# Chunk-contiguous spectra in a fused Fourier / mixture-of-experts / feed-forward kernel

## The chip, the cores and the metric

The kernel runs on one core of a Trainium2 chip. The metric is the device time of one launch in microseconds (us), as a median over runs. Of the five engines, PE multiplies matrices, ACT and VectorE (DVE) do elementwise work and move results out of the accumulator memory (PSUM), POOL does elementwise work on SBUF alone, and SP issues most of the DMAs. "PEld" is PE's loading of the stationary operand, which overlaps its matmuls.

## The reference, cut to what matters

```python
X = np.fft.rfft(x, axis=1)                      # x: 8 x 3072 x 256
Yr = Xr @ w_r - Xi @ w_i + b_r
Yi = Xr @ w_i + Xi @ w_r + b_i
Y  = sign(Y) * max(|Y| - 0.01, 0)               # real and imaginary part apart
x  = np.fft.irfft(Y, n=3072, axis=1).reshape(24576, 256)
# soft mixture of experts: logits = x @ phi; softmax over tokens (dispatch) and over slots (combine);
# 8 experts of two matrices each on 32 slots; then
h  = x @ w_in;  out = (h * tanh(softplus(h))) @ w_out      # 256 -> 2048 -> 256
```

The change is in the first part, between the Fourier transform and the complex product with `w_r` and `w_i`.

## The kernel before, in words

**Two stretches.** The first, up to some 720 us of the trace, runs the Fourier transform, the complex product with its shrinkage, the inverse transform and the softmaxes of the mixture for all 8 sequences, and converts `w_in` and `w_out` on the side. The second, to the end, is the feed-forward part (`ffn`, L797).

**The first stretch by groups.** A sequence is transformed in two stages. `stage1` (L182) is a matrix product over 128 points, whose result goes to memory and comes back in another order (`load_b`, L209). `stage2` (L215) finishes the transform for a group `k` of 8 pairs of frequency blocks; there are 4 groups to a sequence, so 32 in all. Then `linear(k, eh, m)` (L238) makes the complex product in three real products (`m` = 0, 1, 2, with the weights `a`, `b`, `c`) for each half `eh` of the output features, and shrinks the result: ACT evicts `k1`, DVE adds (`p`, L264), ACT makes two one-sided parts (`cl`, `p`, L270 and L271), POOL subtracts them (`yt`, L272). `project` and `inv1` make the logits' share of the group, `ytrans` turns it for later, and `inv2`, `smax1` to `smax3`, `csoft1`, `csoft2`, `fwd1`, `fwd2`, `dturn`, `slots` and `ctrans` work on the softmaxes of a whole sequence.

**The tiles that the change touches.** `stage2` runs for each half `h` of the input features in chunks that start at `p0` = 0, 3 and 6 and hold 3, 3 and 2 pairs: six chunks to a group. A chunk is one PSUM tile `s2` of `n` pairs by 3 parts (real, imaginary, their sum) by 48 frequencies. ACT rounds it into the tile `xh` (L232, to float32r, the type in which the products of `linear` run), and DVE subtracts that from the chunk and writes the remainder into `xl` (L233). Both tiles hold, per half, part by part: 384 real values, 384 imaginary, 384 sums, and two more columns, which are copies (L236) that only the first group of a sequence has. The writes of a chunk therefore go to three places, 384 columns apart. `linear` reads one part as one run of 384 columns, in six matmuls per product (weights high times `xh`, high times `xl`, low times `xh`, for both halves).

**What sets the order.** Each step is put into a list with a position (`at`), the list is sorted, and the instructions are issued in that order: each engine takes its own in order. `stage2(k)` stands at `k` - 1.1, its six chunks one behind the other, before `linear(k-1)`. Waits between engines are placed by the framework, from the stretches of the tiles that the instructions read and write. All PSUM tiles of this stretch come from one pool of 8 banks (`psp`, L104), so PE can start a new tile only when ACT or DVE has read the tile that held the bank.

Of the kernel before, what the change touches and what calls it, by code (L numbers as in the profile page):

```python
# [8 lines left out]
F32 = mybir.dt.float32  # L9
F32R = mybir.dt.float32r  # L10
# [11 lines left out]
NC = 384  # L22
# [8 lines left out]
def constants():  # L31

    n1 = np.arange(N1, dtype=np.float64)
    n2 = np.arange(N2, dtype=np.float64)
    f1 = np.zeros((N1, N1))
    t = np.zeros((96, NP, 96))
    w = 2.0 * np.pi / SEQ
    for i in range(64):
        p, par = divmod(i, 2)
        m, r0, c0 = 2 * i, par * 48, par * 24  # L40
        q = {0: 1, 1: 0}.get(i, i)
        if q:
            ang = 2.0 * np.pi * np.mod(n1 * q, N1) / N1
            f1[:, m], f1[:, m + 1] = np.cos(ang), -np.sin(ang)
            for k2 in range(N2):
                a = w * np.mod(n2 * (q + 128 * k2), SEQ)
                sg = 1.0 if k2 < 12 else -1.0
                t[r0:r0 + 24, p, c0 + k2] = np.cos(a)
                t[r0 + 24:r0 + 48, p, c0 + k2] = np.sin(a)
                t[r0:r0 + 24, p, 48 + c0 + k2] = -sg * np.sin(a)  # L50
                t[r0 + 24:r0 + 48, p, 48 + c0 + k2] = sg * np.cos(a)
        else:
            f1[:, m], f1[:, m + 1] = 1.0, np.where(n1 % 2 == 0, 1.0, -1.0)
            for pos in range(23):
                k, r = (128 * (pos + 1), r0) if pos < 11 else (64 + 128 * (pos - 11), r0 + 24)
                a = w * np.mod(n2 * k, SEQ)
                t[r:r + 24, p, c0 + pos] = np.cos(a)
                t[r:r + 24, p, 48 + c0 + pos] = -np.sin(a)
            t[r0:r0 + 24, p, c0 + 23] = 1.0
            t[r0:r0 + 24, p, 48 + c0 + 23] = np.where(n2 % 2 == 0, 1.0, -1.0)  # L60
    sel = np.tile(np.eye(NS), (4, 1))
    m = np.arange(128).reshape(4, 4, 2, 4)
    order = m.transpose(1, 0, 2, 3).reshape(-1)
    big = np.concatenate([f1, f1.T[order], np.eye(128), sel], axis=1)
    tt = t.transpose(2, 1, 0)
    t3 = np.concatenate([t, t[:, :, 0:48] + t[:, :, 48:96]], axis=2)
    both = np.concatenate([t3.reshape(96, -1), tt.reshape(96, -1)], axis=1)
    return np.ascontiguousarray(big.astype(np.float32)), np.ascontiguousarray(both.astype(np.float32))

# [2 lines left out]
def body(ctx, tc, x, w_r, w_i, b_r, b_i, phi, w1, w2, w_in, w_out, cbig, ct, out, dbg=None, stop=False):  # L72
    nc = tc.nc
# [26 lines left out]
    bp = ctx_r.enter_context(tc.tile_pool(name="bp", bufs=2, side="right"))  # L100
# [5 lines left out]
    def psum(shape, name):  # L106
        return psp.tile(shape, F32, tag="p", name=name)

    tall = const.tile([96, NP * 240], F32, name="tall")
    t_m = tall[:, 0:NP * 144].rearrange("p (n f) -> p n f", f=144)  # L110
# [6 lines left out]
    wsp = {n: (wp.tile([128, 2, D], F32R, name=n + "h"), wp.tile([128, 2, D], F32R, name=n + "l")) for n in "abc"}  # L117
# [8 lines left out]
    x_t, b_t, xh_t, xl_t, yt_t, y_t, pt_t, k1_t = {}, {}, {}, {}, {}, {}, {}, {}  # L126
# [88 lines left out]
    def stage2(k, h, p0):  # L215
        b, g = divmod(k, 4)
        n = min(3, 8 - p0)
        if h == 0 and p0 == 0:
            xh_t[k] = bp.tile([128, 2, 3 * NC + 2], F32R, tag="xh", name="xh")
            xl_t[k] = bp.tile([128, 2, 3 * NC + 2], F32R, tag="xl", name="xl")  # L220
        full = psum([128, 3, 3, 48], "s2")
        ps = full[:, 0:n]
        for i in range(n):
            nc.tensor.matmul(ps[:, i], lhsT=b_t[k][:, p0 + i, h * 128:(h + 1) * 128], rhs=t_m[:, 8 * g + p0 + i, :],  # L224
                             start=True, stop=True)

        def part(t):
            v = t[:, h, 0:3 * NC].rearrange("p (r q f) -> p q r f", r=3, f=48)
            return v[:, p0:p0 + n]

        xh = part(xh_t[k])
        nc.scalar.activation(out=xh, in_=ps, func=AF.Copy)  # L232
        nc.vector.tensor_sub(part(xl_t[k]), ps, xh.bitcast(F32))  # L233
        if g == 0 and p0 == 0:
            for t in (xh_t[k], xl_t[k]):
                nc.vector.tensor_copy(t[:, h, 3 * NC:3 * NC + 2], t[:, h, 47:48 + NC:NC].bitcast(F32))  # L236

    def linear(k, eh, m):  # L238
        if eh == 0 and m == 0:
            pool, tag = (bp, "b") if k >= NK - 2 else (yq, "yq") if k >= NK - 4 else (ytp, "yt")  # L240
            yt_t[k] = pool.tile([128, 2, 8, 2, 48], F32, tag=tag, name="yt")
        xh, xl, yt = xh_t[k], xl_t[k], yt_t[k]
        src, (wh, wl) = ((2, wsp["a"]), (1, wsp["b"]), (0, wsp["c"]))[m]
        w = NC + 2 if m == 0 and k % 4 == 0 else NC
        full = psum([128, NC + 2], "l")
        ps = full[:, 0:w]
        cs = slice(src * NC, src * NC + w)
        es = slice(eh * 128, eh * 128 + 128)
        n = 0
        for h in range(2):  # L250
            for ww, xx in ((wh, xh), (wh, xl), (wl, xh)):
                nc.tensor.matmul(ps, lhsT=ww[:, h, es], rhs=xx[:, h, cs], start=n == 0, stop=n == 5)  # L252
                n += 1
        if m == 0:
            k1_t[eh] = lp.tile([128, NC + 2], F32, tag="k1", name="k1")
            nc.scalar.activation(out=k1_t[eh][:, 0:w], in_=ps, func=AF.Copy)
            if w > NC:
                cs_t[eh] = cs = sm.tile([128, 2, 2], F32, tag="cs", name="cs")
                for i, sc in ((0, 0.5), (1, -0.5)):
                    nc.scalar.activation(out=cs[:, i], in_=k1_t[eh][:, NC:w], func=AF.Relu, scale=sc, bias=half[:, i, eh:eh + 1])  # L260
            return
        ri = m - 1
        p = lp.tile([128, 8, 48], F32, tag="p", name="p")
        nc.vector.tensor_add(p.rearrange("p q f -> p (q f)"), ps, k1_t[eh][:, 0:NC])  # L264
        cl = lp.tile([128, 8, 48], F32, tag="cl", bufs=1, name="cl")
        if k == NK - 1:
            nc.vector.tensor_scalar(cl, p, tlo[:, ri, eh:eh + 1], thi[:, ri, eh:eh + 1], op0=ALU.max, op1=ALU.min)
            nc.vector.tensor_sub(yt[:, eh, :, ri, :], p, cl)
        else:
            nc.scalar.activation(out=cl, in_=p, func=AF.Relu, bias=tup[:, ri, eh:eh + 1])  # L270
            nc.scalar.activation(out=p, in_=p, func=AF.Relu, scale=-1.0, bias=tlo[:, ri, eh:eh + 1])  # L271
            nc.gpsimd.tensor_sub(yt[:, eh, :, ri, :], cl, p)  # L272
        if m == 2 and k % 4 == 0:
            cs = cs_t.pop(eh)
            nc.gpsimd.tensor_sub(yt[:, eh, 0, :, 47], cs[:, 0], cs[:, 1])
# [177 lines left out]
    def evict(b, v, out, ps):  # L453
        if v:
            nc.vector.tensor_copy(out, ps)
        else:
            nc.scalar.activation(out=out, in_=ps, func=AF.Copy)

    def fwd2(b, g):
        dd = ch[b, 0]  # L460
        ps = psum([128, 2, 96], "dt")
        for i in range(2):
            for j in range(4):
                q = 8 * g + 2 * j + i
                nc.tensor.matmul(ps[32 * j:32 * j + 32, i], lhsT=dd[q], rhs=t_m[:, q, 0:96],
                                 start=True, stop=True, tile_position=(0, 32 * j))
        dt = cp.tile([128, 2, 96], F32, tag="pt", bufs=4, name="dtt")
        evict(b, g % 2, dt, ps)
        ch[b, 7, g] = dt
# [100 lines left out]
    for k in range(NK):  # L570
        at(-4 + 0.01 * k if k < 2 else 2.45 if k == 4 else k + PA["lb"], load_b, k)
        for i, (h, p0) in enumerate((h, p0) for h in range(2) for p0 in (0, 3, 6)):
            at(k + PA["s2"] + PA["s2d"] * i, stage2, k, h, p0)
        for i in range(6):
            at(k + i / 6, linear, k, i // 3, i % 3)
        at(k + PA["pj"], project, k)
        at(k + PA["pj"] + 0.3, inv1, k)
        for c in range(4):
            at(k + PA["yt"] + PA["ytd"] * c if k < NK - 4 else NK + TAIL["yt"][k - NK][c], ytrans, k, c)
# [41 lines left out]
    with tc.manual_schedule():  # L621
# [11 lines left out]
        ps = psum([128, 2, NS], "sip")  # L633
# [292 lines left out]
```

## Time and profile before

| | |
|---|---|
| runs | 1980.21, 1981.95, 1984.83 us (median 1981.95) |
| the profiled execution | 1981.18 us, of which the span from first to last instruction is 1979.4 us |
| PE busy | 1922.4 us (97%) |
| DVE busy | 1173.4 us (59%) |
| ACT busy | 892.9 us (45%) |
| POOL busy | 196.9 us (10%) |
| mean granted clock of PE | 0.993 |

The busy time of PE is that of matmuls whose ends are modelled, and they overlap. What PE waits for is read from its idle time, and where that idle time lies from the stretches.

### The profile page before, as it was taken

The page shows a single profiled execution, that of the slowest core. Times are in us where ns is not written, and L with a number is a line of the kernel's source. Part 1 is how long each engine was busy: PE and PEld are TensorE (multiplying, and loading weights), DVE is VectorE, ACT ScalarE, POOL GpSimd, SP SyncE. Part 2 cuts the span into 40 slices and gives each one's busy share as a digit, 9 for nine tenths or more (in the row PEclk, how much of TensorE's full clock was granted, in tenths as well). Part 3 has the DMA queues.
Part 4 walks back from the last instruction along what each step waited for, and adds up shares of the span by engine and source line. Part 5 has one row for each costly group of instructions (what it writes and reads, how often), then busy time and mean ns, then how long its engine had stood idle before and what let it go on. Part 6 is the DMA issues. An engine that isn't in the chain of part 4 may idle for free.

```text
span 1979.4 us, 30141 instructions
## 1 busy us (share of the span) xinstructions
PE 1922.4 (97%) x12226; PEld 1604.8 (81%) x12226; DVE 1173.4 (59%) x1805; ACT 892.9 (45%) x1444; POOL 196.9 (10%) x247
## 2 busy tenths in 40 slices
PE   8899999999998899999999999999999999999999
PEld 5687777777877668888888888888888888888887
DVE  3345555555565656666666666666666666666665
ACT  2666666667666433333333333333333333333332
POOL 0332332333323100000000000000000000000000
PEclk9999999999999999999999999999999999999999
DMA  8655565555542670010002002002001002000000
GB/s 250 216 144 155 158 174 159 157 168 153 170 130 74 250 240 22 22 50 26 22 12 54 22 22 54 22 22 54 22 22 43 22 22 54 22 22 22 22 22 22
DMA packets 92202, 164.26 MB, mean 83 GB/s; under 512 B 27280, under 2 KB 58640, under 8 KB 90016
## 3 DMA queue, kind: packets, MB, share of 16 engines
q1 hardware_dynamic: 90128, 157.45, 26.4%
q0 software_dynamic: 1792, 4.76, 0.7%
q8 instruction: 96, 1.57, 0.3%
q14 instruction: 42, 0.34, 0.1%
q10 hardware_dynamic: 144, 0.13, 0.0%
HBM read 98.75 MB, written 63.57 MB: 82 GB/s over the span
## 4 chain that ended last, share of the span: by engine, by line
PE 82%; ACT 6%; DVE 5%; issue 3%; DMA 2%; POOL 1%; ACTq 0%; SPq 0%; DVEq 0%; POOLq 0%
PE o L858 54%; PE h L828 9%; PE l L252 6%; PE s L224 4%; PE s L195 3%; DVE xl L233 2%; ACT xh L232 2%; PE tr L305 2%; ACT cl L270 1%; ACT p L271 1%; POOL yt L272 1%; PE sps L488 1%; ACT y L310 1%; PE pp L283 1%; DVE p L264 1%
## 5 line engine op out<-in xcount | busy, mean ns | idle before, releaser
L858 PE MATMUL o<-whl,gh 128*128 128x512 f32 x3072 | 1082.9, 395 | 0.0
L858 PE MATMUL o<-whl,gl 128*128 128x256 f32 x3072 | 827.8, 280 | 0.0
L834 ACT ACTIVATE g<-h 128x1024 f32<-128x1024 f32 x384 | 394.3, 1027 | 746.3 <-PE h L828 739.3
L858 PEld LDWEIGHTS o<-whl,gh 128*128 128x128 f32 x3072 | 566.5, 188 | 121.5
L858 PEld LDWEIGHTS o<-whl,gl 128*128 128x128 f32 x3072 | 578.5, 188 | 31.5
L843 DVE TENSOR_TENSOR gl<-g,gh 128x1024 fp32r<-128x1024 f32 x384 | 470.2, 1225 | 28.8 <-DVE gh L839 0.9
L839 DVE CAST gh<-g 128x1024 fp32r<-128x1024 f32 x384 | 265.9, 693 | 351.9 <-ACT g L834 351.8
L828 PE MATMUL h<-ctt,mst 128*128 128x512 f32 x768 | 240.8, 395 | 0.0
L233 DVE TENSOR_TENSOR xl<-s,xh 128x432 fp32r<-128x432 f32 (+1 forms) x192 | 106.1, 558 | 169.2 <-ACT xh L232 169.2
L272 POOL TENSOR_TENSOR yt<-cl,p 128x384 f32<-128x384 f32 x124 | 125.4, 1011 | 399.6 <-ACT p L271 314.3
L224 PE MATMUL s<-tall,bt 96*128 96x144 f32 x1024 | 136.5, 293 | 9.9 <-DMA bt<-sdr 5.4
L224 PEld LDWEIGHTS s<-tall,bt 96*128 96x128 f32 x1024 | 134.7, 197 | 13.7 <-issue 12.2
L232 ACT ACTIVATE xh<-s 128x432 fp32r<-128x432 f32 (+1 forms) x192 | 90.8, 490 | 115.0 <-DVE xl L233 75.9
L828 PEld LDWEIGHTS h<-ctt,mst 128*128 128x128 f32 x768 | 121.2, 188 | 17.9 <-DVE mst L815 0.5
L866 DVE TENSOR_TENSOR os<-o,os 128x256 f32<-128x256 f32 x192 | 76.7, 420 | 77.0 <-ACT os L865 77.0
L270 ACT ACTIVATE cl<-p,tup 128x384 f32<-128x384 f32 x124 | 76.3, 616 | 97.2 <-DVE p L264 69.3
L195 PE MATMUL s<-xc,cb 128*128 128x512 f32 x192 | 104.0, 633 | 8.2 <-DMA xc<-in_x_dram 7.6
L264 DVE TENSOR_TENSOR p<-l,k 128x384 f32<-128x384 f32 x128 | 70.5, 553 | 61.4 <-PE l L252 37.4
L865 ACT ACTIVATE os<-o 128x256 f32<-128x256 f32 x192 | 73.7, 384 | 41.6 <-PE o L858 37.7
L271 ACT ACTIVATE p<-p,tlo 128x384 f32<-128x384 f32 x124 | 76.3, 616 | 4.0
L305 PE MATMUL tr<-cb,yt 128*96 128x128 f32 x512 | 66.6, 276 | 2.9 <-DVE xl L233 1.6
L305 PEld LDWEIGHTS tr<-cb,yt 128*96 128x96 f32 x512 | 53.8, 126 | 18.8 <-DVE xl L233 7.1
(185 smaller groups left out, 1495.8 us busy)
## 6 DMA issues: line engine op xcount, KB each, us to landing
bt<-sdr SPq DMA_DIRECT2D x32, 768.0 KB, 8.0
out_dram<-os SPq DMA_DIRECT2D x47, 512.0 KB, 2.6
xc<-in_x_dram SPq DMA_DIRECT2D x42, 512.0 KB, 5.3
sdr<-a SPq DMA_DIRECT2D x42, 512.0 KB, 3.2
ctt<-c_d SPq DMA_DIRECT2D x28, 384.0 KB, 7.2
c_d<-chl SPq DMA_DIRECT2D x16, 384.0 KB, 3.1
w1t<-in_moe_w_dram SPq DMA_DIRECT2D x6, 1024.0 KB, 6.8
w2t<-in_moe_w_dram SPq DMA_DIRECT2D x5, 1024.0 KB, 10.8
```

The source lines that it names most:

```text
L195: nc.tensor.matmul(ps, lhsT=f1, rhs=xs, start=True, stop=True)
L224: nc.tensor.matmul(ps[:, i], lhsT=b_t[k][:, p0 + i, h * 128:(h + 1) * 128], rhs=t_m[:, 8 * g + p0 + i, :], start=True, stop=True)
L232: nc.scalar.activation(out=xh, in_=ps, func=AF.Copy)
L233: nc.vector.tensor_sub(part(xl_t[k]), ps, xh.bitcast(F32))
L252: nc.tensor.matmul(ps, lhsT=ww[:, h, es], rhs=xx[:, h, cs], start=n == 0, stop=n == 5)
L272: nc.gpsimd.tensor_sub(yt[:, eh, :, ri, :], cl, p)
L305: nc.tensor.transpose(ps[:, i, eh], yt[:, eh, 2 * c + i].rearrange("p r f -> p (r f)"), ident)
L828: nc.tensor.matmul(ps[:, i], lhsT=mst[:, f * 128:f * 128 + 128], rhs=ct_t[b][:, 4 * m:4 * m + 4].rearrange("p n t -> p (n t)"), start=True ...
L834: nc.scalar.activation(out=g, in_=h_t.pop(p), func=AF.Mish)
L839: nc.vector.tensor_copy(gh, g)
L843: nc.vector.tensor_sub(gl, g, gh.bitcast(F32))
L858: nc.tensor.matmul(o, lhsT=a[:, i, ts], rhs=w, start=f == 0 and n == 0, stop=f == 15 and n == 1)
```

## The change

The spectra `xh` and `xl` are laid out with the pair outermost, then the part, then the frequency, where before the part was outermost. A chunk of `stage2` now writes one run of 432 (or 288) columns. The parts stand in the order sum, real, imaginary, for which the constants are put in that order too (`t3`), and `fwd2` reads its two parts from column 48 on. `linear` reads a part as 8 runs of 48 columns, 144 apart, through an access pattern written by hand. The two extra columns become a ninth run of 48, filled with 24 copies of the two values, so the product with `a` in the first group of a sequence has 432 columns where it had 386. The scratch space for POOL's DMAs is halved, as the tiles grow by 46 columns in each half.

```diff
-    t3 = np.concatenate([t, t[:, :, 0:48] + t[:, :, 48:96]], axis=2)
+    t3 = np.concatenate([t[:, :, 0:48] + t[:, :, 48:96], t], axis=2)
...
-            xh_t[k] = bp.tile([128, 2, 3 * NC + 2], F32R, tag="xh", name="xh")
-            xl_t[k] = bp.tile([128, 2, 3 * NC + 2], F32R, tag="xl", name="xl")
+            xh_t[k] = bp.tile([128, 2, 3 * NC + 48], F32R, tag="xh", name="xh")
+            xl_t[k] = bp.tile([128, 2, 3 * NC + 48], F32R, tag="xl", name="xl")
...
         def part(t):
-            v = t[:, h, 0:3 * NC].rearrange("p (r q f) -> p q r f", r=3, f=48)
-            return v[:, p0:p0 + n]
+            return t[:, h, 144 * p0:144 * (p0 + n)].rearrange("p (q r f) -> p q r f", r=3, f=48)
...
-                nc.vector.tensor_copy(t[:, h, 3 * NC:3 * NC + 2], t[:, h, 47:48 + NC:NC].bitcast(F32))
+                nc.vector.tensor_copy(t[:, h, 3 * NC:3 * NC + 48].rearrange("p (a r) -> p a r", r=2),
+                                      t[:, h, 95:144:48][:, None, :].to_broadcast([128, 24, 2]).bitcast(F32))
...
-        src, (wh, wl) = ((2, wsp["a"]), (1, wsp["b"]), (0, wsp["c"]))[m]
-        w = NC + 2 if m == 0 and k % 4 == 0 else NC
-        full = psum([128, NC + 2], "l")
+        src, (wh, wl) = ((0, wsp["a"]), (2, wsp["b"]), (1, wsp["c"]))[m]
+        w, nq = (NC + 2, 9) if m == 0 and k % 4 == 0 else (NC, 8)
+        full = psum([128, NC + 48], "l")
         ps = full[:, 0:w]
-        cs = slice(src * NC, src * NC + w)
+
+        def spec(t, h):
+            v = t[:, h, 48 * src:48 * src + 48]
+            return bass.AP(v.tensor, v.offset, [list(v.ap[0]), [144, nq], [1, 48]])
+
...
-                nc.tensor.matmul(ps, lhsT=ww[:, h, es], rhs=xx[:, h, cs], start=n == 0, stop=n == 5)
+                nc.tensor.matmul(full[:, 0:48 * nq].rearrange("p (q f) -> p q f", f=48), lhsT=ww[:, h, es], rhs=spec(xx, h), start=n == 0, stop=n == 5)
...
-                nc.tensor.matmul(ps[32 * j:32 * j + 32, i], lhsT=dd[q], rhs=t_m[:, q, 0:96],
+                nc.tensor.matmul(ps[32 * j:32 * j + 32, i], lhsT=dd[q], rhs=t_m[:, q, 48:144],
...
-    nc = _bacc.Bacc("TRN2", target_bir_lowering=False, num_devices=1, dynamic_dma_scratch_size=2048)
+    nc = _bacc.Bacc("TRN2", target_bir_lowering=False, num_devices=1, dynamic_dma_scratch_size=1024)
```

No engine's instructions change places. What changes is their shapes and what some of them wait for. On ACT, one group's six chunks of `stage2` and the instruction behind them stand in the order of before like this; `s_833` to `s_866` are the chunks' PSUM tiles, and `PE_49` and `DVE_49` stand for a wait on something that PE or DVE has done:

```order
L232 ACTIVATE xh<-s_833 128x3x3x48 [waits PE_49]
L232 ACTIVATE xh<-s_841 128x3x3x48 [waits DVE_49,PE_49]
L232 ACTIVATE xh<-s_847 128x2x3x48 [waits DVE_49,PE_49]
L232 ACTIVATE xh<-s_852 128x3x3x48 [waits PE_49]
L232 ACTIVATE xh<-s_860 128x3x3x48 [waits DVE_49,PE_49]
L232 ACTIVATE xh<-s_866 128x2x3x48 [waits DVE_49,PE_49]
L256 ACTIVATE k_884<-l 128x384 [waits PE_49]
```

The same place of the changed kernel:

```order
L231 ACTIVATE xh<-s_833 128x432 [waits PE_49]
L231 ACTIVATE xh<-s_841 128x432 [waits PE_49]
L231 ACTIVATE xh<-s_847 128x288 [waits PE_49]
L231 ACTIVATE xh<-s_852 128x432 [waits PE_49]
L231 ACTIVATE xh<-s_860 128x432 [waits PE_49]
L231 ACTIVATE xh<-s_866 128x288 [waits PE_49]
L260 ACTIVATE k_884<-l 128x384 [waits PE_49]
```

Four of the six waited for DVE and no longer do: with the parts outermost, the stretch from the first to the last column of one chunk overlaps that of the next in the same half, so the second chunk's rounding was held until DVE had read the first chunk's. With the pairs outermost the stretches are apart. On PE, the product with `a` of the first group of a sequence (here sequence 0, feature half 0) differs in its width alone:

```order
-L252 MATMUL l<-xh,ah 128x386
-L252 MATMUL l<-xl,ah 128x386
-L252 MATMUL l<-xh,al 128x386
+L256 MATMUL l<-xh,ah 128x432
+L256 MATMUL l<-xl,ah 128x432
+L256 MATMUL l<-xh,al 128x432
```

There are 96 such matmuls in the program; the other 1056 of this line keep their 384 columns.

## Rows read from the trace of the kernel before

**Rows 1.** The page: busy us, share and instructions of each engine
```profile
PE 1922.4 (97%) x12226; PEld 1604.8 (81%) x12226; DVE 1173.4 (59%) x1805; ACT 892.9 (45%) x1444; POOL 196.9 (10%) x247
```

**Rows 2.** Busy us (instructions) of each engine by stretch, clock, DMA share, GB/s
```profile
120.00:650.00 530.00, 502.55 (x4059) 402.13 (x4058) 293.79 (x660) 346.80 (x710) 163.74 (x205) 0.99 0.53 149
...
720.00:1979.00 1259.00, 1254.95 (x6917) 1082.88 (x6915) 798.17 (x967) 466.79 (x581) 0.00 (x0) 1.00 0.10 30
```

**Rows 3.** Waits of PE, 120 to 650 us: us in total, times, longest
```profile
PE l L252 <- DVE rm L330: 8.4, 6, 1.7
PE tn L475 <- ACT dtt L457: 5.9, 5, 1.7
PE dt L465 <- DVE cvc L541: 2.3, 1, 2.3
PE mt L342 <- DVE rm L337: 2.0, 1, 2.0
PE tr L305 <- DVE xl L233: 1.6, 4, 0.6
PE dt L465 <- DMA dd<-ddr: 1.4, 1, 1.4
```

**Rows 4.** Waits of all engines, 120 to 650 us
```profile
ACT xh L232 <- DVE xl L233: 65.7, 89, 1.0
```

**Rows 5.** Timeline of ACT, one group's chunks: start us, us, what, idle before
```profile
401.67 0.54 ACT L232 ACTIVATE xh<-s 128x432 fp32r<-128x432 f32 x1
402.95 0.53 ACT L232 ACTIVATE xh<-s 128x432 fp32r<-128x432 f32 x1 [0.73 <-DVE xl L233]
...
407.06 0.41 ACT L232 ACTIVATE xh<-s 128x288 fp32r<-128x288 f32 x1 [0.73 <-DVE xl L233]
```

**Rows 6.** Timeline of DVE, the same chunks, first and last
```profile
402.25 0.61 DVE L233 TENSOR_TENSOR xl<-s,xh 128x432 fp32r<-128x432 f32 x1 [4.10 <-ACT xh L232]
...
407.50 0.46 DVE L233 TENSOR_TENSOR xl<-s,xh 128x288 fp32r<-128x288 f32 x1 [0.54 <-ACT xh L232]
```

**Rows 7.** Groups by line and shape, DVE: busy us, mean ns, idle before
```profile
L233 DVE TENSOR_TENSOR xl<-s,xh 128x432 fp32r<-128x432 f32 x128 | 77.8, 608 | 134.5 <-ACT xh L232 134.4
...
L264 DVE TENSOR_TENSOR p<-l,k 128x384 f32<-128x384 f32 x128 | 70.5, 553 | 61.4 <-PE l L252 37.4 <-ACT k L256 16.2 <-POOL cvc L543 2.9
L233 DVE TENSOR_TENSOR xl<-s,xh 128x288 fp32r<-128x288 f32 x64 | 29.3, 458 | 34.8 <-ACT xh L232 34.8
...
L236 DVE CAST xh<-xh 128x2 fp32r<-128x2 f32 x16 | 3.0, 185 | 0.0
```

**Rows 8.** Groups by line and shape, ACT
```profile
L232 ACT ACTIVATE xh<-s 128x432 fp32r<-128x432 f32 x128 | 67.6, 528 | 67.7 <-DVE xl L233 31.6 <-PE s L224 23.6 <-DVE xh L236 8.1
...
L232 ACT ACTIVATE xh<-s 128x288 fp32r<-128x288 f32 x64 | 26.4, 412 | 47.3 <-DVE xl L233 44.4 <-PE pp L283 1.5 <-PE s L195 0.7
```

**Rows 9.** The page's groups of the feed-forward part's matmuls
```profile
L858 PE MATMUL o<-whl,gh 128*128 128x512 f32 x3072 | 1082.9, 395 | 0.0
L858 PE MATMUL o<-whl,gl 128*128 128x256 f32 x3072 | 827.8, 280 | 0.0
...
L828 PE MATMUL h<-ctt,mst 128*128 128x512 f32 x768 | 240.8, 395 | 0.0
```

**Rows 10.** Timeline of ACT and DVE, 626 to 630 us
```profile
627.99 1.02 DVE L330 TENSOR_REDUCE rm<-lps 128x32 f32<-128x384 f32 x2 [1.77 <-ACT lg L328]
628.23 2.04 ACT L310 ACTIVATE y<-tr 96x512 f32<-96x512 f32 x4
```

**Rows 11.** Timeline of ACT and DVE, 402 to 416 us
```profile
410.37 2.03 ACT L310 ACTIVATE y<-tr 96x512 f32<-96x512 f32 x4
...
414.28 0.34 DVE L451 SCALAR_TENSOR_TENSOR d_acc<-dtt,ab,d_acc 32x1 f32<-32x1 f32 x1 [3.90 <-ACT dtt L457]
```

**Rows 12.** Timeline of POOL at the start
```profile
4.33 0.72 POOL L143 DMA_DIRECT2D bias<-in_b_i_dram  x1
48.85 1.00 POOL L272 TENSOR_TENSOR yt<-cl,p 128x384 f32<-128x384 f32 x1 [43.81 <-ACT p L271]
```

## The prediction

> **What bounds the kernel now.** I read the engines' busy shares first [rows 1]: PE is busy for 1922.4 of 1979.4 us, the next engine for 59%. So only PE's idle time can be won, 57 us, unless PE's own work changes. The stretches say where it lies [rows 2]: after 720 us PE idles for 4 of 1259 us, and the change touches nothing there. From 120 to 650 us, the steady part of the transform stretch, it idles for 530.00 - 502.55 = 27.45 us. The rest, some 26 us, lies at the start of the stretch, where few groups have begun, and at its end, where the last group's chunks are done; I forecast no change there.
>
> The list of what PE waited for in that part [rows 3] is to be read by the releaser: DVE and ACT instructions, hardly a DMA. The largest, `rm` on DVE with 8.4 us in 6 waits, is a reduction that empties a PSUM bank: PE has run through its eight banks and waits for one. ACT and DVE have far less work than PE in this stretch (346.80 and 293.79 of 530 us), so they are late at certain places only. The wait lists of ACT show one such place [rows 4]: the rounding `xh` waits 89 times for the subtraction `xl`, 65.7 us together. One group's chunks show the mechanism [rows 5, 6]: every second and third chunk of a half waits 0.73 us on ACT, then DVE waits for ACT in turn, so two engines work as one.
>
> **The change part by part.**
>
> *The wait of ACT for DVE.* Four of the six roundings of a group lose it, as the order shows. In the group shown, ACT starts at 401.67 and ends its last chunk at 407.06 + 0.41 = 407.47, DVE at 407.50 + 0.46 = 407.96. Without the waits ACT needs 4 x 528 + 2 x 412 ns = 2.94 us [rows 8] and is done at 404.61, 2.9 us earlier. DVE needs 4 x 608 + 2 x 458 ns = 3.35 us from 402.25 on [rows 6, 7], and is done at 405.60, 2.4 us earlier. It is then DVE that paces the chunks, and ACT is free for `k1`, `cl` and the evictions behind it. So whatever stands behind the chunks on these two queues comes some 2.4 us earlier, where its own input is there.
>
> What is that worth? Only PE's waits count. None of the rows is longer than 2.3 us apiece, within the 2.4 us.
> - Right behind the chunks on ACT or DVE: `rm` (its ACT partner stands a few places behind the last chunk) 8.4, `cvc` 2.3, `xl` 1.6. The smaller rows that I don't show make 27.45 - 21.6 = 5.85 us, most of it waits for `xl`, `k1` and `p`; I take three quarters, 4.4. Together 16.7 us.
> - Further behind: `dtt` 5.9 and the second `rm` (L337) 2.0. Evictions and shrinkages lie between, some of which wait for a product of PE itself and do not move up. Between nothing and 7.9 us I take half, 4.0.
> - The load `dd` (1.4) stays.
>
> That gives -20.7 us, between 0 (if each place only waits for the next thing) and -26.05 (all but the load).
>
> *Two engines reading PSUM at once.* ACT's next chunk will now run beside DVE's last. If that slowed them, the gain would shrink. Four evictions of ACT took 2.04 us beside two reductions of DVE that read PSUM [rows 10], and 2.03 us while DVE stood still [rows 11]. Cost nothing; a bound above is that they take turns again, which is the kernel before.
>
> *One run instead of nine.* DVE's subtraction of 432 columns takes 608 ns in nine pieces; the addition `p`, in one piece, 553 ns for 384 [rows 7]. From 288 to 432 columns it grows by 150 ns, 1.04 a column, so a piece of 384 would be 558 by the strided rows and is 553: the pieces cost about 5 ns, 192 x 5 ns = 1 us of an engine that is 59% busy. I put it at nothing for the end; DVE's slack in rows 2 hides it. [...]
>
> *Wider products.* 96 matmuls of `linear` go from 386 to 432 columns. A column costs (395 - 280) / 256 = 0.449 ns [rows 9]; 96 x 46 x 0.449 ns = 2.0 us, on PE and so on the path. Bounds: 0 if it falls into what is left of PE's idle time, 2.0 otherwise. I take 2.0.
>
> *Broken reads on PE.* All 1152 matmuls of `linear` now read eight or nine runs of 48. The nearest rows are two float32r matmuls of 512 columns: `gh` reads two runs of 256, far apart, `h` one run, and both take 395 ns [rows 9]. A hop there costs under 1 ns. I take 0; the bound above is seven hops of 1 ns, 1152 x 7 ns = 8 us. Nothing suggests that it runs faster.
>
> *The rest.* The copies of L236 grow from 2 to 48 columns: 32 of them, 185 ns before, at most the 458 ns of a 288-column subtraction [rows 7], so under 0.3 us each on DVE in every fourth group: hidden in the 2.4 us. The order of the parts in the constants and in `fwd2` moves no work: 0. POOL's DMA scratch: the only place where several of its DMAs follow each other is the start, the last issued at 4.33 us, and POOL's next work is at 48.85 after 43.81 us of idleness [rows 12]. A stall of several us would be covered; without that cover it would cost its own length.
>
> *The sum.* 1981.18 us is the profiled execution's own time (its span 1979.4, 1.8 around it), 0.8 below the median of the runs. 1981.18 - 20.7 + 2.0 = 1962.5. I say **1962 us**, 1.0% faster.
>
> **The rivals.**
> - *The gaps fill again.* PE arrives earlier at the next late thing, above all the sequence-wide softmax steps, which depend on each other across three engines. For it: `dtt` and L337 belong to such chains. Against it: after the change ACT and DVE have 2.4 to 2.9 us more slack in each of the 32 groups. If only `rm` goes and half of what is close by: -8.4 - 4 + 2 = 1971.
> - *The wait is not what counts.* The removed waits are hidden anyway and the writes were no slower in pieces: 1981 to 1983, the wider products being all that is left. Against it: `rm`, `xl` and `cvc` stand on the chunks' own queue in rows 3.
> - *More than forecast.* A wait shows as idle only beyond the modelled end of the matmul before, 280 - 256 x 0.449 = 165 ns after its columns [rows 9]; 18 waits in rows 3 add 3 us. With all idle time of the part gone: 1981.18 - 27.45 - 3 + 2 = 1953.
> - *Broken reads slow PE* (the slower side). At the pace of `linear` a hop might cost much more than the two-run row shows, as rows 9 hold one hop in 512 columns only. It decides from (20.7 - 2.0) / 1152 = 16 ns a matmul on, 2.3 ns a hop. At 40 ns it costs 46 us: 1962.5 + 46 = 2008.
>
> **How the numbers follow.** Forecast 0.56 (its own range 1957 to 1968); gaps fill again 0.17; more than forecast 0.12; not what counts 0.08; slower reads 0.07. A difference under 0.2% (4 us) can't be told from none. Faster takes the forecast, the third rival and nearly all of the first: 0.84. Same: the second rival in its milder half and a rest of the first, 0.08. Slower: the last and the rest of the second, 0.08. The range for 8 in 10 leaves out the slower reads and most of "not what counts", and a little below 1953: 1953 to 1977.
>
> **What would show it.** In the changed profile the waits of `xh` for `xl` are gone and the chunks of a group take about 3.4 us on DVE, spaced 0.61 apart; PE's waits for `rm` L330 and `xl` nearly vanish; idle time of PE from 120 to 650 us falls from 27 to about 7; the matmuls of 384 columns keep their lengths and spacing, and those of 432 are 20 ns longer; the stretch after 720 us is the same length. I am wrong if PE's idle time stays with other releasers, or if `linear`'s matmuls stand further apart.

## The result, and the profile after

| | kernel before | changed kernel |
|---|---|---|
| median of the runs | 1981.08 us (1975.94 to 1984.83) | 1948.63 us (1945.59 to 1951.73) |
| ratio, 95% interval | | 0.9836 [0.9821, 0.985] |
| span of the profiled execution | 1979.4 us | 1947.2 us |
| mean granted clock of PE | 0.993 | 0.995 |

The change gains 32 us where 19 were forecast, and the time lies below the range that I gave. Timed again beside the last experiments, the changed kernel took 1945.22 us. The mechanism is the one named, the removed waits of ACT; the size is not, and neither is my reason why the new layout removes them.

The page of the changed kernel, in the form of [rows 1]: PE's idle time fell from 57.0 to 1947.2 - 1914.7 = 32.5 us, and its busy time fell too, by 7.7 us, although its matmuls had become wider.

```profile
PE 1914.7 (98%) x12226; PEld 1606.7 (83%) x12226; DVE 1164.5 (60%) x1805; ACT 888.2 (46%) x1444; POOL 195.8 (10%) x247
```

The waits of PE in the changed kernel from 120 to 650 us (total, times, longest), to be held against [rows 3]: `rm` L330 (now L334), `dtt` on ACT, `cvc` and `xl` are gone, what was 8.4 + 5.9 + 2.3 + 1.6 us. Of the rest, `dd`, a load, has grown from 1.4 to 5.7 us.

```profile
PE dt L469 <- DMA dd<-ddr: 5.7, 3, 2.4
PE mt L346 <- DVE rm L341: 1.8, 2, 1.2
PE dps L416 <- ACT dx L375: 0.8, 1, 0.8
PE pp L287 <- POOL yt L276: 0.7, 1, 0.7
PE tn L479 <- DVE dtt L459: 0.2, 1, 0.2
PE lps L331 <- DVE v L322: 0.2, 1, 0.2
```

One group's six chunks, first on ACT, then on DVE, in the form of [rows 5, 6], from two timelines of the changed kernel. Its instructions are now drawn together into one piece, as nothing lies between them: ACT is done with six in 2.41 us, DVE in 2.88 us, where the group shown of before took 5.8 us on ACT. That is less than the 2.94 and 3.35 us of the prediction: it added lengths up, and an instruction here starts before the one ahead of it has ended (ACT's six lengths add up to 4 x 537 + 2 x 430 ns = 3.0 us).

```profile
386.93 2.41 ACT L231 ACTIVATE xh<-s 128x432 fp32r<-128x432 f32 x6
...
387.50 2.88 DVE L232 TENSOR_TENSOR xl<-s,xh 128x432 fp32r<-128x432 f32 x6 [4.10 <-ACT xh L231]
```

The stretches between four places that both programs have: the start of `stage2`'s matmuls of groups 5, 26 and 31, and the first matmul of the feed-forward part. The columns are as in [rows 2]. First the kernel before:

```profile
0.00:118.31 118.31, 99.52 (x550) 76.94 (x551) 43.17 (x96) 52.98 (x103) 24.02 (x34) 0.93 0.71 214
118.31:535.97 417.66, 403.29 (x3246) 321.58 (x3246) 230.22 (x517) 279.09 (x573) 131.29 (x164) 1.00 0.57 161
535.97:637.01 101.04, 90.43 (x731) 73.48 (x731) 58.05 (x131) 61.70 (x126) 30.82 (x39) 0.98 0.41 114
637.01:718.97 81.96, 73.23 (x783) 49.05 (x781) 42.95 (x95) 31.46 (x63) 10.80 (x11) 0.98 0.72 266
718.97:1979.40 1260.43, 1255.98 (x6921) 1083.77 (x6920) 799.01 (x967) 467.64 (x583) 0.00 (x0) 1.00 0.10 31
```

The changed kernel between the same places:

```profile
0.00:114.93 114.93, 99.63 (x550) 78.18 (x551) 42.80 (x96) 53.73 (x103) 24.09 (x34) 0.93 0.74 220
114.93:517.18 402.25, 400.98 (x3246) 323.60 (x3246) 224.72 (x517) 275.48 (x573) 130.00 (x164) 1.00 0.60 167
517.18:606.82 89.64, 86.16 (x732) 72.99 (x731) 54.76 (x129) 59.69 (x125) 30.85 (x39) 1.00 0.47 128
606.82:686.75 79.93, 71.94 (x782) 48.19 (x780) 43.27 (x97) 31.75 (x64) 10.82 (x11) 1.00 0.73 272
686.75:1947.20 1260.45, 1255.96 (x6921) 1083.74 (x6920) 799.00 (x967) 467.57 (x583) 0.00 (x0) 1.00 0.10 31
```

The reader is to subtract the second number from the first of each pair of rows: PE's idle time falls from 14.37 to 1.27 us in the second stretch, from 10.61 to 3.48 in the third, from 18.79 to 15.30 in the first, by 0.74 in the fourth, and not at all in the feed-forward part. PE's busy time falls in the middle three by 2.31 + 4.27 + 1.29 = 7.87 us. The granted clock stands beside it: 0.98 has become 1.00 in two of them. Where it fell is seen in rows of 5 us of the kernel before:

```profile
330.00:335.00 5.00, 3.50 (x44) 2.71 (x44) 2.11 (x6) 3.85 (x9) 2.36 (x4) 0.90 0.82 218
335.00:340.00 5.00, 5.00 (x37) 3.65 (x36) 2.96 (x7) 2.10 (x4) 1.59 (x2) 0.76 1.04 302
630.00:635.00 5.00, 5.00 (x32) 4.35 (x33) 3.69 (x11) 2.93 (x6) 1.23 (x2) 0.66 0.09 30
645.00:650.00 5.00, 2.53 (x37) 1.62 (x36) 3.07 (x8) 2.46 (x5) 0.36 (x1) 0.80 0.43 54
650.00:655.00 5.00, 4.89 (x65) 3.60 (x63) 2.74 (x6) 2.54 (x6) 2.92 (x4) 0.86 0.08 30
```

In the first row PE stands for 1.50 us, before the third for 2.03 us (from 627.6 to 629.63), in the fourth for 2.47, and right there or behind it the clock is below 1.00. A row that is busy for 5 us at 0.66 has lost an estimated 5 x 0.34 = 1.7 us, and that is counted as busy time, since the matmuls then take longer: those of `linear` stand 0.32 us apart behind the first of these stops (from 334.20 us on), and 0.17 to 0.18 us apart just before it. The five rows together lose 0.35 + 1.20 + 1.70 + 0.51 + 0.68 = 4.4 us. In the changed kernel every such row from 105 us to the feed-forward part is at 1.00, also behind its two longest stops there, 2.26 and 2.38 us (up to 549.27 and 618.09). So not each stop is followed by a slower row.

The shapes of the changed kernel, for [rows 7, 8]: `xl` takes 601 and 448 ns (608 and 458 before), `xh` 537 and 430 (528 and 412). PE's 384-column matmul kept its length (342 and 344 before, now 342), and the one of 432 takes 363 where 386 columns took 339. These lengths hold an end that is modelled and overlap the next matmul; what one costs PE is read from start to start, further below.

```profile
L232 DVE TENSOR_TENSOR xl<-s,xh 128x432 fp32r<-128x432 f32 x128 | 73.3, 601 | 92.2 <-ACT xh L231 91.9
L231 ACT ACTIVATE xh<-s 128x432 fp32r<-128x432 f32 x128 | 62.0, 537 | 23.0 <-PE s L224 22.9
...
L232 DVE TENSOR_TENSOR xl<-s,xh 128x288 fp32r<-128x288 f32 x64 | 28.7, 448 | 0.5 <-ACT xh L231 0.5
L231 ACT ACTIVATE xh<-s 128x288 fp32r<-128x288 f32 x64 | 27.5, 430 | 0.9 <-PE s L224 0.9
```

```profile
L256 PE MATMUL l<-xl,ah 128*128 128x384 f32 x96 | 32.8, 342 | 0.0
L256 PE MATMUL l<-xl,ah 128*128 128x432 f32 x32 | 11.6, 363 | 0.0
```

### The profile page after: what moved, and what is told of

It reads as the page before. It is cut to its first block, busy times and chain, and to the rows that moved or that the text cites. A ratio compares the mean times of both kernels' runs of the same rounds, so it can differ in the third digit from the quotient of the medians.

```text
span 1947.2 us, 30032 instructions
## 1 busy us (share of the span) xinstructions
PE 1914.7 (98%) x12226; PEld 1606.7 (83%) x12226; DVE 1164.5 (60%) x1805; ACT 888.2 (46%) x1444; POOL 195.8 (10%) x247
## 4 chain that ended last, share of the span: by engine, by line
PE 92%; DVE 2%; DMA 2%; ACT 2%; issue 1%; POOL 1%; SPq 0%; ACTq 0%; DVEq 0%; POOLq 0%
PE o L862 55%; PE h L832 9%; PE l L256 9%; PE s L224 6%; PE s L195 4%; PE tr L309 3%; PE pp L287 1%; PE sps L492 1%; DMA xc<-in_x_dram 1%; DMA dd<-ddr 1%; PE dt L469 1%; PE iu L298 1%; POOL yt L276 1%; DVE xl L232 1%; PE lps L331 0%
## 5 line engine op out<-in xcount | busy, mean ns | idle before, releaser
L862 PEld LDWEIGHTS o<-whl,gl 128*128 128x128 f32 x3072 | 578.5, 188 | 31.5
L232 DVE TENSOR_TENSOR xl<-s,xh 128x432 fp32r<-128x432 f32 (+1 forms) x192 | 94.5, 550 | 92.7 <-ACT xh L231 92.3
L231 ACT ACTIVATE xh<-s 128x432 fp32r<-128x432 f32 (+1 forms) x192 | 78.4, 501 | 23.9 <-PE s L224 23.8
L314 ACT ACTIVATE y<-tr 96x512 f32<-96x512 f32 x125 | 64.7, 590 | 20.2 <-PE tr L309 20.2
```

The source lines that it names most:

```text
L862: nc.tensor.matmul(o, lhsT=a[:, i, ts], rhs=w, start=f == 0 and n == 0, stop=f == 15 and n == 1)
```

## The experiments

### The waits put back, in all groups and in parts

The changed kernel, with ACT's rounding of every chunk but the first of a half made to wait for the subtraction of the chunk before:

```diff
-        nc.scalar.activation(out=xh, in_=ps, func=AF.Copy)
-        nc.vector.tensor_sub(part(xl_t[k]), ps, xh.bitcast(F32))
+        act = nc.scalar.activation(out=xh, in_=ps, func=AF.Copy)
+        if p0:                       # the parts: k >= 26; k < 5; 5 <= k < 26
+            tc.add_manual_dep(act.ins, last_xl[0], ...)
+        sub = nc.vector.tensor_sub(part(xl_t[k]), ps, xh.bitcast(F32))
+        last_xl[:] = [sub.ins.name]
```

**All groups.** Expected:

> The changed kernel with ACT's four waits for DVE per group put back, layout and all else as changed. Theory (the removed waits are the whole gain): the time goes back to that of before plus at most 2 us for the wider products, 1979 to 1985 us, and PE's waits for rm, dtt, xl and k return, with one to three drops of its clock after 120 us. Rival (the unbroken writes or the new read order bring a part): clearly below 1975 us.

Measured: 1980.92 us (1978.51 to 1982.39), ratio to the kernel before 0.9996 [0.9983, 1.0009]. ACT waits as it did in [rows 4], and DVE's subtraction, with ACT's next rounding held back again, is at 608 and 458 ns as before. PE's waits of [rows 3] return too, and the rows of 5 us fall below 1.00 from 410, 570, 625 and 645 us on, four places where one to three were expected. With everything else of the change in place, putting the four waits of a group back takes the whole gain away.

```profile
ACT xh L232 <- DVE xl L235: 64.2, 87, 1.0
...
PE l L260 <- DVE rm L338: 7.7, 6, 1.7
PE tn L483 <- ACT dtt L465: 5.9, 5, 1.7
```

**Groups 26 to 31.** Expected:

> The waits put back for the last six groups alone (26 to 31). Theory that a wait costs most where the last batches' softmax chains run through the same queues: the 11 to 13 us that the two traces differ by from group 26 on return, 1959 to 1963 us. Rival (each group costs the same): 6 of 32 of the 32 us, so 6 us, 1955 us. Rival (waits are not it): 1949.

Measured: 1961.39 us (1958.97 to 1963.63), ratio 0.9896 [0.9874, 0.9917]. As the theory had it, six groups of 32 cost 12.8 us of the 32: the price of a wait is read from its place, not from a count.

**Groups 0 to 4.** Expected:

> The waits put back for the first five groups alone. Theory: the 3.4 us by which the changed kernel is ahead at the start of group 5 return, 1951 to 1953 us. Rival (that lead comes from the loads, not from the waits): 1948 to 1950. Each group the same: 5 of 32, 1954.

Measured: 1947.62 us (1946.92 to 1949.9), ratio 0.9828 [0.9807, 0.9849]. The theory missed: these waits cost nothing that the runs can tell (the changed kernel's own two medians differ by 3.4 us), so the 3.4 us by which the changed kernel's profile leads at group 5 do not come from them. Over all profiles, group 5 starts at 113.9, 114.3 and 118.3 us in the three kernels with the waits everywhere, at 114.2 in this one, at 108.2 to 114.9 in those that have none so early, and at 116.8 in the one that has them from group 5 on: PE waits there for loads, which land at varying times (the one wait for `bt` there is 5.4 us before and 3.5 in the changed kernel), and 118.3 was a late one.

**Groups 5 to 25.** Expected:

> The waits put back for groups 5 to 25. Theory: the 15.4 us that the two traces differ by in that stretch return, 1962 to 1966 us, of which some 13 show as idle time of PE and some 2 do not. Rival (each group the same): 21 of 32, 1970. If the three parts add up to the whole, the stretches do not pass lateness on to each other.

Measured: 1965.99 us (1963.71 to 1969.05), ratio 0.9922 [0.9904, 0.994], so 17.4 us, near the upper end of what the theory had; PE's idle time from group 5 on is 24.7 us in this profile and 12.7 in the changed kernel's. The three parts give 12.8 - 1.0 + 17.4 = 29.2 us of the 32.3 that all together cost, the same to within the 3.4 us above.

### The old layout with wider tiles

Meant to price the wider products and the smaller scratch alone: the kernel before, parts outermost, with the changed kernel's widths.

```diff
-            xh_t[k] = bp.tile([128, 2, 3 * NC + 2], F32R, tag="xh", name="xh")
-            xl_t[k] = bp.tile([128, 2, 3 * NC + 2], F32R, tag="xl", name="xl")
+            xh_t[k] = bp.tile([128, 2, 3 * NC + 48], F32R, tag="xh", name="xh")
+            xl_t[k] = bp.tile([128, 2, 3 * NC + 48], F32R, tag="xl", name="xl")
...
-        cs = slice(src * NC, src * NC + w)
+        cs = slice(src * NC, src * NC + wm)     # wm: 432 where w was 386
...
-    nc = _bacc.Bacc("TRN2", target_bir_lowering=False, num_devices=1, dynamic_dma_scratch_size=2048)
+    nc = _bacc.Bacc("TRN2", target_bir_lowering=False, num_devices=1, dynamic_dma_scratch_size=1024)
```

> The kernel before with two side effects of the change alone: the product with a in the first group of each sequence has 432 columns where it had 386, and POOL's DMA scratch is halved; the layout and the waits are those of before. Theory: 96 products 20 ns longer on PE, plus 2 us, 1982 to 1984 against 1981. Rival (PE has slack there, or the columns are hidden): no difference. Rival (the scratch stalls POOL): several us more, with POOL's DMA issues longer at the start.

Measured: **1943.57 us** (1941.01 to 1944.5), ratio 0.9808 [0.9794, 0.9821]. Every expectation missed. In the order of its instructions none of the six chunks waits for DVE, though each still writes three places 384 columns apart. So the layout is not needed to lose the waits. From here on the question was what places them. The price of the wider products is read from the starts of PE's matmuls below.

### Two columns more, three columns more

The kernel before with nothing changed but the width of its two tiles per half: 1156 columns, then 1157, in place of 1154. The new columns are never touched.

```diff
-            xh_t[k] = bp.tile([128, 2, 3 * NC + 2], F32R, tag="xh", name="xh")
-            xl_t[k] = bp.tile([128, 2, 3 * NC + 2], F32R, tag="xl", name="xl")
+            xh_t[k] = bp.tile([128, 2, 3 * NC + 4], F32R, tag="xh", name="xh")      # + 5: 1157
+            xl_t[k] = bp.tile([128, 2, 3 * NC + 4], F32R, tag="xl", name="xl")      # + 5: 1157
```

The order of ACT's instructions, second and third chunk, at 1156 and then at 1157 columns:

```
L232 ACTIVATE xh<-s_841 128x3x3x48 [waits PE_49]
L232 ACTIVATE xh<-s_847 128x2x3x48 [waits PE_49]

L232 ACTIVATE xh<-s_841 128x3x3x48 [waits DVE_49,PE_49]
L232 ACTIVATE xh<-s_847 128x2x3x48 [waits DVE_49,PE_49]
```

**1156 columns.** Expected:

> The kernel before with its layout, its 386-column products and its scratch, and only its two tiles 1156 instead of 1154 columns wide per half; the two new columns are never touched. In the order of its instructions ACT's four waits for DVE in a group are gone all the same. My theory (these waits are the whole gain, and the framework's test of overlapping stretches places them at some widths of the tile and not at others): 1940 to 1947 us, at least as fast as the changed kernel. Rival (part of the gain comes from the unbroken runs, or from the smaller scratch): 1953 to 1970. Rival (the 432-column products cost nothing): the same as the version with tiles of 1200 columns, 1943.6; if they cost their 2 us, 1941.6.

**1157 columns.** Expected:

> As the run with 1156 columns per half, but 1157: one column more. In the order of its instructions ACT's four waits in a group are back. My theory (the waits alone): 1979 to 1984 us, like the kernel before. Rival (a wider tile is itself faster, by where its columns lie): 1940 to 1950.

Measured: 1156 columns 1944.77 us (1944.12 to 1947.02), ratio 0.9826 [0.9811, 0.9841]; 1157 columns 1980.34 us (1976.28 to 1984.51), ratio 1.0001 [0.9991, 1.0011]. One column decides over 35 us, through the waits alone. At 1157 ACT waits as in [rows 4]:

```profile
ACT xh L232 <- DVE xl L233: 67.1, 91, 1.0
```

Both times came as my theory had them. At 1156 columns PE's largest waits from 120 to 650 us are those of the changed kernel:

```profile
PE dt L465 <- DMA dd<-ddr: 5.7, 3, 2.5
PE mt L342 <- DVE rm L337: 2.3, 2, 1.7
```

The chunks' columns are apart in memory at every width, so the wait protects nothing: the framework's test for overlapping stretches doesn't find them apart at some widths. In the old layout the order, built at 27 widths, has the waits at 1154, 1157, 1159, 1162, 1163, 1166, 1174, 1175, 1190, 1198, 1202 and 1210 columns, and not at 1155, 1156, 1158, 1160, 1161, 1164, 1167, 1168, 1170, 1172, 1173, 1180, 1194, 1200 and 1204. No width of the first list is a multiple of 3 or of 4, and each of the second is. That is a pattern of these 27 orders; why the test follows it isn't shown, and only 1154, 1156, 1157 and 1200 were timed. In the new layout, where a chunk is one unbroken run, it has them at none of six widths from 1200 to 1215.

### The changed kernel again, and with unbroken reads

Run side by side with the two above: the changed kernel itself, and a version whose product reads one run of 384 columns in place of 8 runs of 48 (it reads columns that are not the part's).

```diff
-            v = t[:, h, 48 * src:48 * src + 48]
-            return bass.AP(v.tensor, v.offset, [list(v.ap[0]), [144, nq], [1, 48]])
+            v = t[:, h, NC * src:NC * src + 48]
+            return bass.AP(v.tensor, v.offset, [list(v.ap[0]), [48, nq], [1, 48]])
```

The changed kernel again. Expected:

> The changed kernel itself, on the same chip as the three others of this call, to see how much of the 5 us between it and the old layout with wide tiles is there when both are timed side by side. My theory (the two have the same waits, so what differs is how often the clock falls in an execution): 1944 to 1952 us, and its interval overlaps that of the kernel with 1156 columns plus 2 us. Rival (broken reads, or the constants' order): 4 us or more above it.

Unbroken reads. Expected:

> The changed kernel, but the complex product reads each part as one run of 384 (or 432) columns, as before, which are not the part's columns; all instructions and shapes stay. If PE's reads in eight runs of 48 cost nothing, as the durations of the products say (342 to 344 ns in both kernels): 1946 to 1952 us, the same as the changed kernel. Rival (the changed kernel stands some 5 us above the one with the old layout and 1200 columns because of these reads): 1941 to 1945.

Measured: the changed kernel 1945.22 us (1944.19 to 1947.17), ratio 0.9827 [0.9812, 0.9842]; with unbroken reads 1944.64 us (1944.23 to 1949.85), ratio 0.983 [0.9813, 0.9847]. By these medians neither the reads nor the layout makes a difference, but 1944.64 also lies in the rival's range, and the traces decide for the rival. Between group 5 and the feed-forward part both kernels have the same idle time of PE and the clock at 1.00 throughout, and PE is busy for 3.0 us less with unbroken reads. First the changed kernel again, then the unbroken reads:

```profile
113.30:684.96 571.66, 559.01 (x4757) 444.82 (x4756) 323.92 (x742) 366.98 (x760) 171.52 (x213) 1.00 0.60 176
...
113.53:682.22 568.69, 556.02 (x4758) 442.36 (x4757) 322.41 (x742) 366.67 (x760) 171.72 (x213) 1.00 0.60 176
```

From the start of one of `linear`'s matmuls to the next it takes 178.3 ns at 384 columns with broken reads and 175.3 with unbroken ones (means at the full clock, without the places where PE does something else first). So 1152 broken reads cost some 3.4 us. That the medians don't show it fits the clock: the mean granted clocks of the runs with unbroken reads are 0.993 to 0.996, those of the changed kernel 0.996 to 0.998. The two profiled executions, both at 0.996, took 1944.41 us with unbroken reads and 1947.17 with broken ones.

The 0.45 us between the new layout and the old one with two unused columns more hide the same. Matched matmul by matmul from group 5 to the feed-forward part, the new layout takes 4.8 us more at the full clock, for its broken reads and wider products, and the old one lost 4.4 us in this profile, where its clock fell at three places (0.993 to 0.995 over its runs):

```profile
113.70:684.81 571.11, 558.24 (x4757) 444.84 (x4756) 322.47 (x742) 366.08 (x760) 171.62 (x213) 0.99 0.59 176
```

### Broken writes in the new layout

Each run of 48 gets two unused columns behind it, so that a chunk again writes nine (or six) runs, and the waits stay away.

```diff
-            return t[:, h, 144 * p0:144 * (p0 + n)].rearrange("p (q r f) -> p q r f", r=3, f=48)
+            return t[:, h, 150 * p0:150 * (p0 + n)].rearrange("p (q r f) -> p q r f", r=3, f=50)[:, :, :, 0:48]
```

> The changed kernel with two unused columns behind each run of 48 in xh and xl, so a chunk writes nine runs with gaps and no longer one, while the chunks' stretches stay apart and no wait comes back. Theory (the waits are the gain): 1946 to 1951 us, the same as changed, with xl and xh within 10 ns of the changed kernel's. Rival (the unbroken run itself brings a part): above 1955 us.

Measured: 1951.32 us (1945.72 to 1956.34), ratio 0.9841 [0.9824, 0.9859]; `xl` 600 and 447 ns, `xh` 537 and 430. The unbroken write itself brings nothing: what a chunk takes on the two engines is the same, hops between its runs or not (601 and 448, 537 and 430 in the changed kernel). The median is 0.3 us above what the theory had, and PE's reads can explain it: in runs 150 columns apart a matmul of `linear` takes 182.7 ns from start to start where the changed kernel's takes 178.3, 5 us over 1152 of them.

### What is late next: the load `dd`

Its 5.7 us are the largest wait that the changed kernel has left there. Two runs move it. The first has `fwd2`, which reads `dd`, and `dsum` 0.1 later in the list of positions:

```diff
-... ds=2.47, ... f2=2.46 ...
+... ds=2.57, ... f2=2.56 ...
```

> The changed kernel with fwd2 and what hangs on it placed 0.1 of a group later for all but the last batch. It aims at what PE waits for now, the load dd (5.7 us in 3 waits). Theory: these waits go, 2 to 5 us less, 1944 to 1947 us. Rival (something else is late there then): 1948 to 1950.

Measured: 1950.01 us (1946.9 to 1954.84), ratio 0.9845. The wait went and another came, as PE's waits show: no gain.

```profile
PE tn L479 <- DVE dtt L459: 5.5, 5, 2.6
...
PE dt L469 <- DMA dd<-ddr: 0.5, 2, 0.3
```

The second issues the load behind the one of `bt` on SP's queue, to see what a long wait of PE costs:

```diff
-... dl=2.05 ...
+... dl=2.12 ...
```

> The changed kernel with the load dd issued one place later, behind the next group's bt load, so that PE gets a wait of a few us once per batch, 7 in all; nothing else changes. It asks what a wait costs beside its idle time. Theory: the time rises by more than PE's idle time does, by some 0.17 us per wait that is hidden behind the matmuls in flight and by the slow clock if it drops (half of the time at the lower level). Rival: the time rises by the idle time alone.

Measured: 1991.7 us (1990.19 to 1995.41), ratio 1.0057 [1.0043, 1.0072]: 43 us slower than the changed kernel. PE's wait for `dd` from 120 to 700 us grew by 29.5 us:

```profile
PE dt L469 <- DMA dd<-ddr: 35.2, 7, 7.4
```

The rest is the clock. Matched matmul by matmul from group 5 to the feed-forward part, this profile is 47.7 us longer than the changed kernel's: 29.3 us are PE's idle time, 18.2 lie where the granted clock was low. After one of these waits (4.46 us, ending at 421.45) the rows of 5 us of this kernel read:

```profile
420.00:425.00 5.00, 3.55 (x38) 2.97 (x38) 0.83 (x3) 0.33 (x1) 0.61 (x1) 0.60 0.98 294
425.00:430.00 5.00, 5.00 (x47) 3.50 (x50) 3.27 (x7) 1.20 (x3) 0.00 (x0) 0.50 0.66 137
430.00:435.00 5.00, 5.00 (x42) 4.17 (x42) 1.99 (x6) 3.00 (x6) 1.01 (x1) 0.88 0.01 3
```

The granted clock goes to 0.50, the lowest in any row of these runs, while PE works again, and by the estimate above these three rows lose 3.55 x 0.40 + 5 x 0.50 + 5 x 0.12 = 4.5 us beside the 4.46 that PE stood. Both rows of the kernel before from 420 to 430 us are at 1.00.

## Why the prediction was wrong in its size

**The account over several traces.** A single pair of profiles carries the luck of its start. So I take the span from the start of group 5 on, PE's idle time from 120 to 760 us, and the clock's loss there (over rows of 5 us, busy time x (1 - granted clock)), for the three profiles that have ACT's waits in all groups, then six that have none and keep the places of all steps, then the one with the long waits for `dd`:

| profile | span from group 5 | PE idle | clock's loss |
|---|---|---|---|
| before | 1861.1 | 33.7 | 4.4 |
| waits put back | 1863.8 | 30.0 | 8.8 |
| old layout, 1157 columns | 1866.3 | 32.0 | 12.7 |
| changed | 1832.2 | 12.7 | 0.0 |
| changed, again | 1832.1 | 12.6 | 0.0 |
| unbroken reads | 1829.1 | 12.7 | 0.0 |
| old layout, 1156 columns | 1831.5 | 12.9 | 4.5 |
| old layout, 1200 columns | 1831.0 | 12.9 | 1.7 |
| broken writes | 1841.5 | 11.0 | 8.2 |
| load behind | 1880.0 | 42.0 | 20.3 |

The means of the three and of the six are 1863.7 and 1832.9, 30.8 us apart: 31.9 - 12.5 = 19.4 us of idle time, 8.6 - 2.4 = 6.2 us of clock, and 5.2 us that these two columns don't hold. The last row lies 47.8 us above the changed kernel's, and the columns hold 29.3 + 20.3 = 49.6: the clock's column is somewhat too high, as `linear`'s matmuls in that profile's row at 0.50 (425 to 430 us) stand 0.32 us apart, not twice 0.18. The three and the six mix the two layouts, whose own work for PE differs by 4.8 us; the bullet on waits behind matmuls splits a pair of one layout.

- **What bounds the kernel: the step that failed.** "So only PE's idle time can be won, 57 us, unless PE's own work changes" took the idle time that the profile shows for the whole price of a stop, and a stop cost more in two ways. PE's work took longer where the clock fell (those 0.32 us for 0.18), and it fell behind some of the stops. I read the granted clock as 0.99 in [rows 2] and gave it no price: this term of the sum was 0 and measured some 6 us, 4.4 in the two profiles of the first table. The long waits for `dd` show the same from the other side. And a part of each stop lies under the modelled end of the matmul before it, 5 to 6 us here, which I left out of the sum (below).
- **Which stops bring the clock down is open.** Rows fell behind stops of 1.50 and 2.03 us of the kernel before, and stayed at 1.00 behind one of 2.38 us (up to 618.09) of the changed kernel. From group 5 on the clock fell at 3, 4 and 6 places in the three profiles with the waits, and at 0, 0, 0, 3, 1 and 2 in the six without. What decides isn't shown, so this term is in part luck.
- **The wait term.** Its sum was right, the way to it only partly. I forecast 20.7 us of idle time from 120 to 650; from group 5 to the start of group 31 (118 to 637 us of before) it fell by 13.10 + 7.13 = 20.23, and by 0.74 behind that. I had taken three quarters of the small waits and half of `dtt` and L337. `dtt`, `rm` L330 and the small ones went whole, and in exchange `dd`, which I had said stays at 1.4, rose by 4.3: a part of the rival in which the gaps fill again.
- **No change at start and end.** Right for the end (0.74 us of idle time, and the feed-forward part is as long to 0.02 us). The 3.5 us at the start of the shown profile are scatter of the loads, as the waits put back early show.
- **Waits behind matmuls still in flight.** The rival "more than forecast" priced them at 165 ns each, 3 us for 18. The starts of PE's matmuls, compared place by place, bear the price out. The kernel with the waits put back has 32 stops, at the full clock, where the changed kernel has none; each delays the next matmul by 174 ns, on average, more than its idle time shows, 5.6 us together. The kernel before has 34, at 175 ns, 6.0 us. From group 5 to the feed-forward part the waits put back cost 31.5 us: 17.3 of idle time, 5.1 more at the same stops (net of those that only the changed kernel has), 0.9 in delays too short to show as idle, and 8.2 where the clock was low. The price was right; the number of stops was counted too low, and the sum left it out.
- **Wider products.** 2.0 us forecast and found: at 432 columns 197.1 ns from start to start (unbroken reads), at 386 columns 177.0 (before), 96 x 20.1 ns = 1.9 us.
- **Broken reads.** Put at 0, with 8 us as the bound; they cost 3.0 ns a matmul, 3.4 us. The row that they were put at 0 by has one hop in a matmul, these have seven, at 0.4 ns each. It is the rival "broken reads slow PE" at a small size, and it made the gain smaller, not larger.
- **One run in place of nine, two engines on PSUM, scratch: 0 each.** Right for the first, by its own run. Beside DVE, `xh` became 9 and 18 ns longer, 4 x 9 + 2 x 18 = 72 ns a group on an engine with slack. The scratch was not tried alone; with it at its old size, the old layout at 1156 columns has the whole gain.
- **Why the waits go.** That a chunk's stretch from first to last column overlaps the next one's in the old layout is true, but isn't what places the waits: at 1156 columns the stretches overlap as much. The kernel before has a width at which the test fails. The new layout is one way to be safe from it, two unused columns another, in the same time by the medians and with 4.8 us less work for PE from group 5 on.

By the medians none of the versions beats the changed kernel by more than the runs scatter: 1943.57 us for the old layout with 1200 columns, 1944.77 with 1156, 1945.22 for the changed kernel beside the latter.

## What to carry to other kernels

When an engine waits for another between two pieces of a tile that don't touch the same columns, look at the waits in the order of instructions for some other widths of the tile before moving data: here two unused columns gave what a new layout gave. Price a wait of PE at its idle time, at what the modelled end of the matmul before hides (here 174 and 175 ns a stop), and at the granted clock behind it, read in short rows; here the clock added a third of the idle time that went, and two thirds where the stops were long. Take the account from several profiles, since the start of one differed by up to 10 us from that of another, and compare starts of matmuls at the full clock before calling two medians the same: falls of the clock hid 3 to 5 us twice.

## What the runs showed of the hardware

A stop of PE of 1.50 us (up to 332.84 us of the kernel before) was followed by a row at 0.76, a stop of 4.46 us (load behind) by rows at 0.50 and 0.88, and stops of 2.26 and 2.38 us (changed kernel) by none below 1.00. A rounding of ACT took 537 and 430 ns while DVE read PSUM beside it (changed kernel), where it took 528 and 412 in turns (before), whereas DVE's own instruction became shorter, 601 for 608 and 448 for 458. A matmul of PE with a float32r operand in 8 runs of 48 columns, 144 apart, took 178.3 ns from start to start where one run of 384 took 175.3 (unbroken reads), and 182.7 with the runs 150 apart (broken writes).
